# Sparse attention and a two-layer FFN: q and k on 128 partitions, one score phase, finer loads, stores on another queue

## The chip, the cores and the metric

The kernel runs on one core of a Trainium2 chip. The metric is the device time of one execution in microseconds, median of several runs. The profile gives the span from the first to the last instruction, which is some 2 us shorter than the device time here (313.7 us timed, 311.9 us span in the profiled run of the kernel before). A run that is over 1.5% above the fastest of its kernel counts as slow and is to be left out. Spans and lengths of stages are read from one profiled run per kernel.

The engines: PE (TensorE matmul), ACT (ScalarE), DVE (VectorE), POOL (GpSimd), SP (SyncE, here only a queue that issues DMA).

## The reference

```python
q, k, v: (8, 8, 576, 64)                    # batch, heads, tokens, head dim
rel = pos[:, None] - pos[None, :]
mask_local   = (rel >= 0) & (rel < 32)                        # heads 0 to 3
mask_strided = (rel >= 0) & (pos[None] % 32 == pos[:, None] % 32)   # heads 4 to 7
attn = softmax(where(mask, q @ k.T / 8, -1e9)) @ v
x    = attn as (8*576 tokens, 512)
out  = (((x @ w1) * (x @ w2)) @ w3) @ w_out                   # 512 -> 1024 -> 1024 -> 512
```

Both kernels fold `w3 @ w_out` into one matrix `w34` first, so that a token needs three products. Both compute only the blocks that the masks leave: six blocks of 96 queries by 128 keys for a local head, eight blocks of 72 by 72 for a strided head. Work is in fp16 with fp32 accumulation.

## The kernel before

The parts that the change and the argument touch, cut:

```python
LQ, LT = 96, 6          # local heads: 96 partitions, 6 tokens each
SQ, ST = 72, 8          # strided heads: 72 partitions, 8 tokens each
stgp = pool("stgp", bufs=5)                # fp32 staging, 8 KB slots
qkp  = pool("qkp", bufs=1)                 # cast q and k
psF  = pool("psF", bufs=3, PSUM)           # FFN and fold accumulators, one bank each
psB  = pool("psB", bufs=2, PSUM)           # scores and P*V, two banks each
psM  = pool("psM", bufs=1, PSUM)           # everything that is transposed, one bank

def load_w12():                            # 512 columns of w1 or w2 at a time
    ...
            nc.sync.dma_start(st, wd...)
            nc.scalar.copy(out=wh[:, 0:1, cs], in_=st[:, 0:1, :])
            nc.vector.tensor_copy(out=wh[:, 1:KM, cs], in_=st[:, 1:KM, :])

def ph_T(s, which):                        # one phase for q, one for k, of a head pair
    ps = psM.tile([P, 1024], FP16, tag="m")
    for c in range(n):                     # n = 6 or 8, w = 96 or 72
        pe(nc.tensor.transpose(ps[:, c * w:(c + 1) * w], src[:, c]..., id16[0:w, 0:w]))
    # one copy out of PSUM: q on ACT, k on DVE; POOL clears the pad behind k

def ph_S(s, g):                            # scores of half a pair's blocks, two phases a pair
    sps = psB.tile([P, 2, 512], FP32, tag="big")
    # m blocks x 2 heads: matmuls with 64 rows
    nc.scalar.activation(out=pte, in_=sps, func=AF.Exp, scale=scale)
    nc.vector.tensor_mul(ptm, pte, mask)

def ph_PV(s, g): ...                       # P*V, then reciprocal and product on DVE -> xqs
def ph_T2(s): ...                          # transposes xqs into xT, the FFN's input

# order of phases for pair p: S(p,0) Tq(p+1) S(p,1) T2(p-1) PV(p,0) Tk(p+1) PV(p,1)
# FFN tile t (512 tokens) is 16 first-layer units and 8 output units, four matmuls of
# 512 columns each; the phases of batch t+1 are laid between the units of tile t
```

The kernel keeps PE's instructions in program order (`pe(...)` in the listing), so a phase whose input is late holds up everything behind it. A "bank" below is a PSUM buffer of 2 KB a partition, as these pools allot them.

The softmax here doesn't subtract the row's maximum and nothing guards it: scores larger than these inputs give would overflow.

## Time and profile before

| | before |
|---|---|
| device time, median | 312.58 us (3 runs, 311.95 to 314.9) |
| first FFN matmul | 65.44 us |
| FFN tile 0 | 29.56 us |
| a steady FFN tile (tiles 1 to 5) | 28.71 us |
| first matmul of tile 7 (the last two tiles carry no attention) | 266.00 us |
| span | 311.9 us |

The starts of tiles are read from the timeline: the first `aps` matmul after an output unit.

Part 2 of the page, 40 slices of 7.8 us each; digits are tenths:

```profile
PE   0285757689999999999999999999999999999994
...
PEclk9999897569999999999999999999999999999999
DMA  6999999998769989999895868660002001102003
```

PE is full from the tenth slice on. Before that it is half empty, while the DMA engines are busy all the time (a share of 0.94 to 1.10 in every 10 us from 10 to 70 us), and the clock that PE is granted sinks to 0.5. At 0.5 the first unit of four FFN matmuls takes 1.71 us (65.64 us), at full clock 0.86.

The windows view of three stretches: the attention of batch 0, tile 0, a steady tile. Columns: stretch, its length, busy time (and count) of PE, PEld, DVE, ACT, POOL, then granted clock, DMA share, GB/s.

```profile
29.90:65.40 35.50, 24.89 (x282) 15.93 (x282) 24.71 (x44) 15.13 (x25) 12.55 (x24) 0.75 1.00 249
65.44:95.01 29.57, 29.57 (x296) 15.31 (x294) 20.95 (x40) 13.95 (x25) 17.82 (x27) 0.96 0.80 177
152.42:181.13 28.71, 28.45 (x298) 14.84 (x295) 20.52 (x41) 14.27 (x25) 11.95 (x21) 1.00 0.79 196
```

The chain of waits, start, length and what; first two links in the head, then three of a steady tile:

```profile
44.13 1.66 DVE w1h L141
56.35 1.66 DVE w2h L141
...
128.38 0.23 PE sps L224 x6
128.62 0.97 PE aps L294 x4
129.58 0.26 PE ps L201 x8
```

In the head, two casts of weights on DVE are links of the chain: batch 0's attention waits in the same queue. In the steady tile, all links are PE.

### The profile page before, as it was taken

The page shows a single profiled execution, that of the slowest core. Times are in us where ns is not written, and L with a number is a line of the kernel's source. Part 1 is how long each engine was busy: PE and PEld are TensorE (multiplying, and loading weights), DVE is VectorE, ACT ScalarE, POOL GpSimd, SP SyncE. Part 2 cuts the span into 40 slices and gives each one's busy share as a digit, 9 for nine tenths or more (in the row PEclk, how much of TensorE's full clock was granted, in tenths as well). Part 3 has the DMA queues.
Part 4 walks back from the last instruction along what each step waited for, and adds up shares of the span by engine and source line. Part 5 has one row for each costly group of instructions (what it writes and reads, how often), then busy time and mean ns, then how long its engine had stood idle before and what let it go on. Part 6 is the DMA issues. An engine that isn't in the chain of part 4 may idle for free.

```text
span 311.9 us, 6533 instructions
## 1 busy us (share of the span) xinstructions
PE 277.8 (89%) x2561; PEld 144.2 (46%) x2561; DVE 188.9 (61%) x361; ACT 134.6 (43%) x221; POOL 100.3 (32%) x192
## 2 busy tenths in 40 slices
PE   0285757689999999999999999999999999999994
PEld 0133334554554554555455554555554555444441
DVE  1234378868767676777678566778765666442421
ACT  2323435345545544544454455445544543332330
POOL 5041520557463364435356171733230000000000
PEclk9999897569999999999999999999999999999999
DMA  6999999998769989999895868660002001102003
GB/s 227 371 228 324 229 376 232 177 210 150 183 165 261 196 189 248 226 182 206 243 223 113 217 191 159 143 187 36 0 36 101 2 3 74 62 0 101 35 2 136
DMA packets 48287, 50.23 MB, mean 161 GB/s; under 512 B 26496, under 2 KB 32640, under 8 KB 48256
## 3 DMA queue, kind: packets, MB, share of 16 engines
q1 hardware_dynamic: 48256, 49.82, 63.1%
q8 instruction: 20, 0.33, 0.5%
q14 instruction: 11, 0.09, 0.1%
HBM read 40.37 MB, written 9.44 MB: 160 GB/s over the span
## 4 chain that ended last, share of the span: by engine, by line
PE 83%; DVE 6%; ACT 5%; DMA 3%; issue 1%; SPq 0%; DVEq 0%; ACTq 0%
PE ops L317 26%; PE bps L303 20%; PE aps L294 20%; PE ps L201 5%; PE sps L224 5%; PE xps L250 4%; DMA st<-in_moe_w_dram 3%; PE ps L266 3%; ACT pte L229 2%; DVE w_115 L350 1%; ACT xT_112 L273 1%; DVE w3T_117 L346 1%; DVE xqs L258 1%; PE ps L344 1%; DVE t L212 1%
## 5 line engine op out<-in xcount | busy, mean ns | idle before, releaser
L297 ACT COPY asb<-aps 128x512 f32<-128x512 f32 x72 | 42.2, 586 | 68.8 <-PE aps L294 51.3
L229 ACT ACTIVATE pte<-sps 128x576 f16<-128x576 f32 (+1 forms) x64 | 41.6, 650 | 36.7 <-PE sps L224 36.1
L173 POOL CAST t<-st 72x1024 f16<-72x1024 f32 x32 | 33.0, 1059 | 25.0 <-DMA st<-in_q_dram 15.1
L258 DVE TENSOR_TENSOR xqs<-xps,rcp 96x384 f16<-96x384 f32 (+1 forms) x64 | 39.6, 619 | 2.1
L154 POOL CAST t<-st 96x768 f16<-96x768 f32 x32 | 26.9, 867 | 29.2 <-DMA st<-in_q_dram 17.1
L303 PEld LDWEIGHTS <-w2h 128*128 128x128 f16 x288 | 24.5, 98 | 22.1 <-issue 1.3
L294 PEld LDWEIGHTS <-w1h 128*128 128x128 f16 x288 | 24.6, 99 | 21.9 <-issue 0.6
L201 PEld LDWEIGHTS <-t 72*128 72x128 f16 (+1 forms) x448 | 25.1, 101 | 17.0 <-issue 4.0
L201 PE MATMUL ps<-id_79,t 72*128 72x72 f16 (+1 forms) x448 | 28.5, 206 | 3.1 <-ACT w3T_118 L347 2.8
L250 PEld LDWEIGHTS <-ptm 72*128 72x128 f16 (+1 forms) x448 | 23.2, 101 | 17.2 <-issue 2.2
L236 DVE TENSOR_TENSOR ptm<-pte,maskS 72x576 f16<-72x576 f16 x32 | 19.3, 603 | 17.7 <-ACT pte L229 17.5
L294 PE MATMUL aps<-xT_112,w1h 128*128 128x512 f16 x72 | 27.5, 382 | 1.6 <-ACT xT_112 L273 1.5
L232 DVE TENSOR_TENSOR ptm<-pte,maskL 128x576 f16<-128x576 f16 x32 | 18.4, 576 | 16.2 <-ACT pte L229 15.6
L294 PE MATMUL aps<-xT_109,w1h 128*128 128x512 f16 x72 | 27.8, 386 | 0.0
L303 PE MATMUL bps<-xT_109,w2h 128*128 128x512 f16 x72 | 27.6, 384 | 0.0
L294 PE MATMUL aps<-xT_111,w1h 128*128 128x512 f16 x72 | 27.5, 382 | 0.0
L294 PE MATMUL aps<-xT_110,w1h 128*128 128x512 f16 x72 | 27.5, 382 | 0.0
L303 PE MATMUL bps<-xT_110,w2h 128*128 128x512 f16 x72 | 27.3, 379 | 0.0
L303 PE MATMUL bps<-xT_112,w2h 128*128 128x512 f16 x72 | 27.3, 379 | 0.0
L303 PE MATMUL bps<-xT_111,w2h 128*128 128x512 f16 x72 | 27.2, 378 | 0.0
L329 ACT COPY osb<-ops 128x512 f32<-128x512 f32 x18 | 10.5, 586 | 33.0 <-PE ops L317 33.0
L224 PEld LDWEIGHTS <-t 64*128 64x128 f16 x448 | 11.1, 97 | 29.1 <-issue 22.5
(89 smaller groups left out, 415.0 us busy)
## 6 DMA issues: line engine op xcount, KB each, us to landing
st<-in_q_dram SPq DMA_DIRECT2D x16, 576.0 KB
st<-in_k_dram SPq DMA_DIRECT2D x16, 576.0 KB
out_dram<-osb SPq DMA_DIRECT2D x36, 256.0 KB
st<-in_moe_w_dram SPq DMA_DIRECT2D x8, 1024.0 KB
st<-in_v_dram SPq DMA_DIRECT2D x32, 160.0 KB
st<-in_v_dram SPq DMA_DIRECT2D x8, 576.0 KB
st<-in_moe_w_out_dram SPq DMA_DIRECT2D x2, 1024.0 KB
st<-in_v_dram SPq DMA_DIRECT2D x8, 128.0 KB
```

Source lines behind the costliest of these rows:

```text
L154: nc.gpsimd.tensor_copy(out=t[:, hp], in_=stv[:, 2 * hp:2 * hp + 2].rearrange("p h c d -> p c h d"))
L173: nc.gpsimd.tensor_copy(out=t[:, hp], in_=stv[:, 2 * hp:2 * hp + 2].rearrange("p h c d -> p c h d"))
L201: pe(nc.tensor.transpose(ps[:, c * w:(c + 1) * w], src[:, c].rearrange("p h d -> p (h d)"), id16[0:w, 0:w]))
L224: pe(nc.tensor.matmul(sps[:, h, i * w:(i + 1) * w], s.tT["k"][r, ks:ks + P], s.tT["q"][r, w * t:w * t + w], start=True, stop=True))
L229: nc.scalar.activation(out=pte[0:kr], in_=sps[0:kr, :, 0:288], func=AF.Exp, bias=0.0, scale=scale)
L236: nc.vector.tensor_mul(ptm[0:kr, 0:576].rearrange("p (a x) -> p a x", x=w), pte[0:kr].rearrange("p h (a x) -> p (h a) x", x=w), _ap(maskS, ...
L250: pe(nc.tensor.matmul(xps[:, h, i * 65:(i + 1) * 65], ptm[0:kr, c0:c0 + P], vt[0:kr, 2 * (s.hp % 2) + h, g * m + i, :], start=True, stop=T ...
L258: nc.vector.tensor_mul(xqs[0:w, 0:m].rearrange("p i h d -> p h i d"), xv[:, :, :, 0:D], _ap(rcp, 0, [[rp, w], [4, 2], [1, m], [0, D]]))
L294: pe(nc.tensor.matmul(aps, w1h[:, ci, bass.ds(jc * P, P)], xT[ci][:, tok], start=(ci == 0), stop=(ci == KM - 1)))
L297: nc.scalar.copy(out=asb, in_=aps)
L303: pe(nc.tensor.matmul(bps, w2h[:, ci, bass.ds(jc * P, P)], xT[ci][:, tok], start=(ci == 0), stop=(ci == KM - 1)))
L317: pe(nc.tensor.matmul(st["ps"], lhs(ci), rhs(ci), start=(ci == 0), stop=(ci == KF - 1)))
```

## The change

Its intent: split every head's 576 tokens into 512, loaded as 4 tokens on each of 128 partitions, and a rest of 64. Then q and k of a pair, 512 columns each, fill the one PSUM bank that the kernel has for transposes (`psM`, 1024 fp16), and one phase transposes both. The rests of all heads are transposed once per batch. Scores become one phase a pair. Loads are cut to at most 512 KB over nine 4 KB slots, casts in the head are spread over ACT, DVE and POOL, cast q and k are double-buffered, and output tiles are copied by ACT and stored from ACT's queue. The core of the diff, cut:

```diff
-    stgp = ctx.enter_context(tc.tile_pool(name="stgp", bufs=5))
-    qkp = ctx.enter_context(tc.tile_pool(name="qkp", bufs=1))
+    stgp = ctx.enter_context(tc.tile_pool(name="stgp", bufs=9))
+    qkp = ctx.enter_context(tc.tile_pool(name="qkp", bufs=2))
...
+    def load_qk(b, grp, engs="pp"):
+        for nm, ten, eng in (("q", q, engs[0]), ("k", k, engs[1])):
+            st = stgp.tile([P, 4, 4, D], FP32, tag="stg")
+            nc.sync.dma_start(..., ten[b, 4 * grp:4 * grp + 4, 0:NM].rearrange("h (p c) d -> p h (c d)", c=4))
+            copy(eng, t, st.rearrange("p h c d -> p c h d"))
...
-    def ph_T(s, which):
+    def ph_T(s):
+        ps = psM.tile([P, 2, NM], FP16, tag="m")
+        for i, nm in enumerate("qk"):
+            for c in range(4):
+                pe(nc.tensor.transpose(ps[:, i, c * P:(c + 1) * P], ..., id16))
+        # then q out of it on ACT, k on DVE
+    def ph_R(b): ...                       # the 64 rest tokens of all heads: 4 transposes, 4 copies
-    def ph_S(s, g):
+    def ph_S(s):
+        for g in range(2):
...
-                if ts % 2 == 0:
-                    nc.scalar.copy(out=osb, in_=ps)
-                else:
-                    nc.vector.tensor_copy(out=osb, in_=ps)
-                nc.sync.dma_start(out_r[tch * (NT // P) + ts], osb)
+                nc.scalar.copy(out=osb, in_=ps)
+                nc.scalar.dma_start(out_r[tch * (NT // P) + ts], osb)
...
-    host(later, 14)
-    att_only(batch_end[0])
+    host(fold, 8, lead=14)                 # 14 fold units first, then 8 phases among the rest
+    host([lambda: None], batch_end[0])     # the rest of batch 0 alone
+    host(ab_halves(0), pos[0] + 6, lead=8) # 6 phases of batch 1 in the last 8 first-layer units
+    host(o_halves(0), batch_end[1])        # 15 or so in the 8 output units
```

Also cut: local v is loaded once and its overlapping rows are copied by DVE (`L180` below) instead of being loaded twice; masks shrink; pads are cleared once.

## The prediction

> **What bounds the kernel now.** From 65.6 us to the last matmul (307.8 us) TensorE is the limit. The windows view of one steady stage (one 512-token FFN tile with one batch of attention laid between, 28.7 us) shows PE busy 28.44 of 28.70 us, clock 1.00, DVE 20.0, ACT 14.3, POOL 13. In the chain of waits such a stage is PE throughout: 96 matmuls of 512 columns at 0.216 us = 20.7 us, and about 7.5 us of attention. The head, 0 to 65.6 us, is not PE-bound: its PE work is about 26 us (64 fold matmuls 13.8, fold transposes 3.6, one batch of attention 7.5, a start on the next), so some 39 us are lost. There the DMA share is 0.8 to 1.1 in every 10 us window, PE waits 8.4 us for the first w3 cast (first transpose at 13.05), the clock falls to 0.6 at 48 to 66 us, and the last w2 cast ends at 58. The load queue also waits for casts to free staging slots.
>
> **What the change does.**
> - Head: w3 first, in 512 KB pieces over nine small staging slots, w_out and w3 before q, k, v; casts spread over three engines; batch 1 after w1/w2. First transposes at about 6.5 us instead of 13, fold done by about 25. Needed before the first FFN tile: 10.5 MB of weights and 3.5 MB of batch 0. The trace moves 290 to 300 GB/s in 0 to 48 us (weights near 400, 72- and 96-partition loads 190 to 250), so 14 MB take 47 to 50 us. [...] Against that, q/k and w1/w2 packets shrink to 1 KB; by the trace's packet times I estimate 60 ns each, 290 GB/s.
> - Attention of batch 0 ends near 42 to 45 us, w1/w2 complete near 50; the first FFN tile starts at 46 to 48, fed in four pieces. Batch 1 lands after 60, so tile 0 carries 2 to 4 us of stalls.
> - Steady: columns transposed for q and k stay 4608 a batch, so PE saves only 0.1 us there; one score phase saves one of two 0.1 us entry gaps, 0.4 us a batch. 28.7 becomes about 28.2: 3.5 us over seven stages. POOL memsets, mask and copy changes are off the path. Output copies and store issues move to ACT (+1.2 us copies, about 1.6 us issue per stage): ACT near 60%, hidden.
> - Tail: 41.4 us for the last two tiles, plus 4 us, unchanged.
>
> **Sum.** Start of first tile 47 + 9 tiles 186 + seven batches at 7.1 = 50 + stalls 4 + tail 4 = 291 us. About 19 us of the gain is the head, 3 the stages.
>
> **What shows it right.** First FFN matmul at 45 to 52 us; first transpose before 8; stages of 28.0 to 28.4; DMA share above 0.9 until about 60 us; fewer clock drops in the head. [...] this trace has 0.5 at 54 to 68 us, where PE is sparse.
>
> **What makes it wrong.** 1 KB packets slower than estimated; batch 1 starved in tile 0; ACT blocked behind a store; the score phase waiting for both PSUM buffers; slow POOL casts delaying batch 0.
>
> Faster by over 2% 0.94, within 2% 0.05, slower 0.01; range 281 to 302.

Beside its two estimates, the profile of the kernel before shows these numbers: for 60 ns a packet, 48256 packets that took 63.1% of 16 engines' span of 311.9 us, 65 ns on average at 1.03 KB; for 1.6 us of issue a stage (four stores), 0.33 us in the median and 0.82 at most for one issue.

## The result, and the profile after

The changed kernel takes 301.51 us (4 runs, 300.88 to 302.47) against 313.27 us for the kernel before in the same rounds (4 runs). The ratio is 0.9625, 95% interval 0.9568 to 0.9682. Ratios here are the mean time of one kernel's fast runs over that of the other's fast runs of the same rounds, so not quite the ratio of the medians.

It is faster, as forecast, and the time lies in the range, but only 0.5 us below its upper end and 10.5 us above the point.

| stage (us) | before | sum in the prediction | after |
|---|---|---|---|
| first FFN matmul | 65.44 | 47 | 51.10 |
| tile 0 | 29.56 | 20.7 + 7.1 + 4 = 31.8 | 36.12 |
| tiles 1 to 6 | 170.99 | 6 x 27.8 = 166.8 | 165.94 |
| last two tiles and tail | 45.9 | 41.4 + 4 | 45.4 |
| span | 311.9 | 291 | 298.5 |
| time of the profiled run | 313.7 | 291 | 300.9 |

So the start of the FFN is 4.1 us later than predicted and tile 0 is 4.3 us longer; the steady tiles are right to a microsecond, the tail too. The last 2.4 us are the step from span to time, which the sum left out.

The page's part 2 after:

```profile
PE   1396677999889999999999999999999999999995
...
PEclk9999995899999999999999999999999999999999
DMA  7999997696289998997699894120011002003003
```

PE is full from the eighth slice, sags once at slices 11 and 12, and the clock sinks for two slices instead of four. The windows view after: fold, attention of batch 0, tile 0, a steady tile (columns as before):

```profile
12.16:27.10 14.94, 13.66 (x88) 7.56 (x88) 6.74 (x13) 7.23 (x10) 3.97 (x5) 1.00 1.15 317
27.10:51.10 24.00, 16.33 (x208) 10.34 (x208) 18.94 (x41) 11.45 (x19) 7.33 (x8) 0.85 1.01 288
51.10:87.22 36.12, 32.03 (x308) 17.06 (x306) 25.67 (x52) 19.88 (x36) 17.02 (x18) 0.96 0.71 176
170.96:198.79 27.83, 27.53 (x277) 14.93 (x274) 19.42 (x42) 15.14 (x30) 9.25 (x10) 1.00 0.49 124
```

The stretch of batch 0's attention takes 24.0 us instead of 35.5. The two don't hold quite the same work: the stretch before also has 32 matmuls of the fold and the first phases of batch 1 (PE busy 24.9 us), the one after 24 matmuls of the fold (PE busy 16.3 us). Tile 0 is 8.3 us longer than a steady tile. The scores in the chain of waits of a steady tile:

```profile
176.72 0.36 PE sps L246 x12
177.08 0.97 PE bps L319 x4
```

Twelve score matmuls in 0.36 us and one slowed group behind them, where before six took 0.23 us and each six had its slowed group.

The timeline in tile 0 shows what is new. Columns: start, length, engine, line, operation, count, and in brackets how long the engine had been idle and what ended it. `ps` is the bank for transposes; the 4 transposes at L228 are those of the rests.

```profile
61.27 0.61 PE L212 MATMUL ps<-id_79,t 128*128 128x128 f16 x8
...
61.91 0.58 ACT L68 COPY qT<-ps 128x512 f16<-128x512 f16 x1 [0.72 <-PE ps L212]
...
62.53 0.69 DVE L70 COPY kT<-ps 128x512 f16<-128x512 f16 x1 [0.30 <-ACT qT L68]
...
63.27 0.38 PE L228 MATMUL ps<-id_79,t 128*128 128x128 f16 x4 [0.54 <-DVE kT L70]
```

(L68, L70 and L72 are the lines of a helper that copies on ACT, DVE and POOL; the names of the tiles tell the copies apart.) The copy of k starts only when that of q has ended (0.62 us after it started), and the next transposes wait for the copy of k. The two copies read different halves of the same PSUM bank. It is so in the whole trace: of 15.8 us that DVE sat idle before such copies in this kernel, 15.3 ended with ACT's copy of q. Why the second copy waits was not shown, since no run gave q and k a bank each; with the layout that lets them share one, their copies run in series.

The first transposes did come early, at 5.32 us. The timeline shows what became of that:

```profile
5.32 1.04 PE L355 MATMUL ps<-id_79,t 128*128 128x128 f16 x8 [2.25 <-POOL t L72]
...
10.46 0.69 DVE L70 CAST woh<-st 128x1024 f16<-128x1024 f32 x1 [1.85 <-DMA st<-in_moe_w_out_dram]
11.07 0.42 DVE L357 COPY w3T_129<-ps 128x512 f16<-128x512 f16 x1
...
12.16 1.01 PE L355 MATMUL ps<-id_79,t 128*128 128x128 f16 x8 [5.80 <-ACT w3T_130 L358]
```

DVE has two casts of w_out ahead of the copy of those transposes and waits for their loads. PE's second block starts at 12.16 us; the first block of the kernel before started at 13.06.

### The profile page after: what moved, and what is told of

The parts are those of the page before. It is cut to its first block, busy times and chain, and to the rows that moved or that the text cites. A ratio compares the mean times of both kernels' runs of the same rounds, so it can differ in the third digit from the quotient of the medians.

```text
span 298.5 us, 6146 instructions
## 1 busy us (share of the span) xinstructions
PE 269.3 (90%) x2401; PEld 143.0 (48%) x2401; DVE 183.5 (61%) x382; ACT 145.7 (49%) x256; POOL 86.5 (29%) x102
## 4 chain that ended last, share of the span: by engine, by line
PE 62%; DMA 18%; DVE 7%; ACT 6%; POOL 3%; issue 3%; SPq 1%; POOLq 0%; ACTq 0%
PE ops L333 17%; PE bps L319 16%; PE aps L310 15%; DMA st<-in_v_dram 10%; PE xps L266 4%; PE ps L212 3%; DMA st<-in_moe_w_out_dram 3%; DMA out_dram<-osb 3%; PE sps L246 2%; DMA st<-in_k_dram 2%; DVE kT L70 2%; ACT qT L68 2%; PE ps L282 2%; DVE xqs L274 1%; ACT pte L251 1%
## 5 line engine op out<-in xcount | busy, mean ns | idle before, releaser
L72 POOL CAST t<-st 128x1024 f16<-128x1024 f32 (+1 forms) x40 | 39.7, 994 | 74.6 <-DMA st<-in_q_dram 29.6
L251 ACT ACTIVATE pte<-sps 128x576 f16<-128x576 f32 (+1 forms) x64 | 38.3, 648 | 11.0 <-PE sps L246 11.0
L68 ACT COPY qT<-ps 128x512 f16<-128x512 f16 (+1 forms) x48 | 22.8, 481 | 31.9 <-PE ps L212 27.4
L344 ACT COPY osb<-ops 128x512 f32<-128x512 f32 x36 | 21.1, 585 | 28.5 <-PE ops L333 28.5
L70 DVE COPY kT<-ps 128x512 f16<-128x512 f16 (+1 forms) x48 | 25.2, 538 | 15.8 <-ACT qT L68 15.3
L310 PE MATMUL aps<-xT_121,w1h 128*128 128x512 f16 x72 | 27.6, 384 | 0.0
L212 PE MATMUL ps<-id_79,t 128*128 128x128 f16 x256 | 19.5, 219 | 1.7 <-ACT w3T_130 L358 1.3
L212 PEld LDWEIGHTS <-t 128*128 128x128 f16 x256 | 16.5, 98 | 9.1 <-issue 2.5
L272 DVE RECIPROCAL rcp<-xps 96x6 f32<-96x6 f32 (+1 forms) x64 | 12.2, 190 | 12.6 <-PE xps L266 12.3
L282 PEld LDWEIGHTS <-xqs 72*128 72x128 f16 (+1 forms) x224 | 12.5, 100 | 9.8 <-issue 2.0
L282 PE MATMUL ps<-id_79,xqs 72*128 72x72 f16 (+1 forms) x224 | 14.5, 206 | 2.8 <-DVE kT L70 1.9
```

Of the source, the lines that this page charges most:

```text
L68: nc.scalar.copy(out=out, in_=in_)
L70: nc.vector.tensor_copy(out=out, in_=in_)
L72: nc.gpsimd.tensor_copy(out=out, in_=in_)
L212: pe(nc.tensor.transpose(ps[:, i, c * P:(c + 1) * P], src[:, c, h0:h0 + 2].rearrange("p h d -> p (h d)"), id16))
L251: nc.scalar.activation(out=pte[0:kr], in_=sps[0:kr, :, 0:288], func=AF.Exp, bias=0.0, scale=scale)
L282: pe(nc.tensor.transpose(ps[:, t * w:(t + 1) * w], s.xqs[t // m][0:w, t % m].rearrange("p h d -> p (h d)"), id16[0:w, 0:w]))
```

## The experiments

Twelve more kernels were run. All but two (e6 and e12) give the right result. Starts and lengths of tiles are from each run's timeline.

| run | first FFN matmul | tile 0 | tiles 3 to 5, each | span | ratio to before |
|---|---|---|---|---|---|
| changed kernel | 51.10 | 36.12 | 28.12, 27.84, 27.83 | 298.5 | 0.9625 |
| e1_spread | 50.88 | 35.73 | 28.03, 27.83, 27.83 | 298.5 | 0.9576 |
| e2_two_scores | 51.10 | 34.25 | 28.89, 28.89, 28.89 | 302.8 | 0.9717 |
| e3_stores_sp | 50.01 | 36.33 | 27.61, 27.83, 27.61 | 297.8 | 0.9578 |
| e4_single_casts | 51.25 | 36.56 | 28.21, 27.83, 27.83 | 299.2 | 0.9592 |
| e5_old_layout | 50.00 | 37.37 | 28.12, 31.77, 27.91 | 304.7 | 0.9761 |
| e6_quarter_w12 | 57.00 | 36.28 | 27.83, 27.83, 27.83 | 304.9 | one look |
| e7_batch0_first | 53.11 | 34.70 | 28.57, 27.84, 27.83 | 299.4 | 0.9652 |
| e8_two_m | 47.05 | 34.48 | 28.54, 28.36, 27.87 | 298.1 | 0.9570 |
| e9_shared_banks | 47.38 | 35.78 | 27.83, 27.83, 27.83 | 295.0 | 0.9384 |
| e10_shared_batch0 | 56.68 | 34.76 | 28.22, 27.83, 27.83 | 303.7 | 0.9588 |
| e11_relief | 47.20 | 35.87 | 27.83, 27.83, 27.83 | 295.2 | 0.9374 |
| e12_light_pool | 46.64 | 33.21 | 27.83, 27.93, 27.83 | 292.3 | 0.9405 |

The intervals of the ratios reach about 0.003 to 0.009 to either side, and the chips differ, so ratios less than one per cent apart are not told apart here. By the two per cent rule every kernel with a ratio is faster than the kernel before, except e5, which is unclear (0.9706 to 0.9815). In the rounds of e9 to e11 the record lists three of the seven runs of the kernel before as slow, and the ratios seem to include them; against the four fast ones e9 is 0.944, which is still below the changed kernel's interval.

Stage lengths in the profiles repeat to a few hundredths of a microsecond where PE is full, and tell more. Starts and spans repeat less well. The four timed runs of one kernel have spans that differ by 0.7 us (e8) to 5.0 us (e10); for the changed kernel they run from 298.5 to 300.3. The profile is one of these runs: the fastest for the changed kernel and e12, the slowest for e9, e10 and e11. A difference of a microsecond or two in a start or a span is therefore weak evidence. Tile 0 also holds a stretch at half clock whose length varies: 3.1 us in the changed kernel, none in e7, 6.1 us in e10.

### e1_spread: is batch 1's attention squeezed into too few units?

```diff
-    host(ab_halves(0), pos[0] + 6, lead=8)
+    host(ab_halves(0), pos[0] + 12, lead=2)
```

> The changed kernel with batch 1's attention laid from the second unit of FFN tile 0 on (12 of its phases in the first 14 units left, the rest in the output half) instead of 6 phases in the last 8 units. In the changed kernel tile 0 takes 36.1 us (51.1 to 87.2) against 27.8 for a later tile. Theory A, the attention is squeezed: 15 phases between 8 output units wait for each other's copies, so spreading them makes tile 0 about 30 to 32 us and the span 4 to 6 us shorter (about 293). Rival B, batch 1's data come late: the PE then waits for q, k and v inside the first half of tile 0 instead, and tile 0 stays at 35 to 37 us.

Measured: tile 0 takes 35.73 us, the span is the same 298.5. Theory A fell: more units between the phases bought nothing. Rival B is not borne out either: PE's waits in tile 0 name no load. The main ones are these (engine, line, waited for: us, times, longest):

```profile
PE xps L266 <- DVE ptm L253: 1.4, 2, 0.9
PE ps L212 <- DVE kT L70: 1.4, 2, 1.2
PE ps L228 <- DVE kT L70: 1.1, 1, 1.1
```

The copy of k out of the shared bank, and the mask product `ptm` on DVE. Both became the next theories.

### e2_two_scores: what is one score phase worth?

```diff
-            add(ph_S, pairs[p])
+            add(ph_S, pairs[p], (0,))
+            add(ph_S, pairs[p], (1,))
```

(with `ph_S` taking the groups as an argument, and the counts of phases before tile 0 and in it raised to match)

> The changed kernel with the scores in two phases again. Theory: one phase saves one entry gap of PE, 0.09 us a pair, 0.36 us a batch; so a steady tile goes from 27.84 to about 28.2 us, and the span by 2.5 to 3 us to 301 to 302. Rival: the steady gain (28.71 to 27.84) is from elsewhere (q/k layout or stores), and the steady tile stays below 27.95.

Measured: a steady tile takes 28.89 us instead of 27.83, so one score phase is worth 1.05 us a tile, not the 0.36 expected. The chain of waits of this run:

```profile
177.41 0.23 PE sps L246 x6
177.65 0.97 PE aps L310 x4
178.62 0.23 PE sps L246 x6
178.85 0.97 PE bps L319 x4
```

Two phases cost 2 x (0.23 + 0.11 that the unit behind is longer) = 0.68 us a local pair; one costs 0.36 + 0.11 = 0.47. That is 0.21 us a pair, 0.84 a batch. The other 0.2 us of a tile are a wait at its start, for ACT's copy of `xT`; in the waits view over four tiles, first e2, then the changed kernel:

```profile
PE aps L310 <- ACT xT L289: 2.0, 4, 0.5
PE aps L310 <- ACT xT_124 L289: 1.2, 4, 0.3
```

The prediction had counted one 0.1 us a pair. There are two: of the second group's 0.23 us only 0.13 are work (0.36 less 0.23), and the unit behind it is 0.11 longer. Scores use 64 rows, the FFN matmuls before and behind them 128; this trace puts the cost of going from one to the other at about 0.1 us on each side. What causes it was not shown.

Tile 0 tells the opposite: with two score phases it takes 34.25 us, 1.9 less than in the changed kernel, at the same start and with as long a stretch at half clock. So the single phase wins 1.05 us in every steady tile and loses some of it where PE waits for ACT and DVE; on the span it is worth 4.3 us.

### e3_stores_sp and e4_single_casts: stores and the double buffer

```diff
-                nc.scalar.copy(out=osb, in_=ps)
-                nc.scalar.dma_start(out_r[...], osb)
+                if ts % 2 == 0: nc.scalar.copy(...)
+                else: nc.vector.tensor_copy(...)
+                nc.sync.dma_start(out_r[...], osb)
```

> The changed kernel with the output tiles copied by ACT and DVE in turn and stored from the queue that also issues the loads, as before. Theory: stores and copies lie off the path in a steady tile; 27.84 us a tile stays within 0.15 us, and the span within 1.5 us of 298.5 (perhaps shorter, as ACT has less to do). Rival: the split of the queues matters, loads wait behind stores, and steady tiles lengthen by over 0.3 us.

```diff
-    qkp = ctx.enter_context(tc.tile_pool(name="qkp", bufs=2))
+    qkp = ctx.enter_context(tc.tile_pool(name="qkp", bufs=1))
```

> The changed kernel with one buffer instead of two for the cast q and k. Theory: loads and casts run far ahead of the attention in steady tiles, so nothing there changes (27.84 within 0.15); batch 1's casts must wait for batch 0's transposes, which are long over, so the span stays within 1 us of 298.5. Rival: the double buffer carries part of the gain, and the span grows by 2 us or more.

Measured: 297.8 and 299.2 us of span, steady tiles of 27.6 to 27.8 us and 27.8. Neither part carries any of the gain that can be seen. e4 stays within what its theory said. e3 does nearly: two of its steady tiles are 27.61 us, 0.23 shorter than 27.84 where 0.15 was allowed, and tile 1 is longer, 28.53 us instead of 27.78.

### e5_old_layout: what is the layout worth?

```diff
-            st = stgp.tile([P, 4, 4, D], FP32, tag="stg")        # 128 partitions, 4 tokens
+                st = stgp.tile([w, 2, n * D], FP32, tag="stg")   # 96 x 6 or 72 x 8, two heads
-    def ph_T(s):  ...
+    def ph_T(s, nm): ...          # q and k in two phases, as before; no ph_R
```

(eight staging slots instead of nine, because the cast tiles of this layout are larger)

> The changed kernel with q and k loaded and transposed as before (96 and 72 partitions, a transpose phase each for q and k, none for the rest), one staging slot less so that it fits. Theory: the layout is worth 0.1 to 0.3 us in a steady tile, and shows in the head, where each phase costs a copy: tile 0 then starts at 53 to 57 us instead of 51.1, the span is 4 to 8 us longer. Rival: the head is bound by what is loaded; the layout moves fewer packets per byte before, so the head does not change by over 1 us.

Measured: the first FFN matmul at 50.0 us, a microsecond earlier, so the layout is not what shortened the head; tile 0 at 37.37, 1.25 us longer. Tile 1 takes 28.90 us, 1.1 more; tiles 2, 3 and 5 take 27.9 to 28.25 us, up to 0.4 more. The span is 6.2 us longer, of which 3.9 are in one tile. The timeline shows it:

```profile
174.14 0.59 ACT L324 COPY osb<-ops 128x512 f32<-128x512 f32 x1 [1.46 <-DMA out_dram<-osb]
...
175.32 0.38 PE L290 MATMUL aps<-xT,w1h 128*128 128x512 f16 x1 [1.86 <-ACT xT L269]
```

ACT waited for an earlier store to free an output buffer, the copy of `xT` stood behind it in ACT's queue, PE stood still for 1.86 us, and the clock was at half for the next 3.4 us. This is the "ACT blocked behind a store" of the prediction. It did not happen in the changed kernel; whether the layout or chance brought it on is open, since this is one profile.

### e6_quarter_w12: does loading bound the start of the FFN?

```diff
+            if g == 0:
+                w12st[eng] = consts.tile([P, KM, 256], FP32, name="w12st" + eng)
+                nc.sync.dma_start(w12st[eng], ...)
-            copy(eng, wh[:, :, cs], st)
+            copy(eng, wh[:, :, cs], w12st[eng])
```

> Wrong result on purpose: only the first quarter of w1 and w2 is loaded and cast four times, 3 MB less to load in the head (one staging slot less, so that it fits). If loading bounds the start of the first FFN tile, it starts some 8 to 10 us earlier than 51.1. If the chain of batch 0's attention does, it stays within 1.5 us of 51.1; batch 1's data would then land some 8 us earlier, and tile 0 is shorter than 36.1 us only if it was starved by them.

Measured: with 3 MB less to load, the first FFN matmul came 5.9 us later, at 57.0. So less to load did not help. The timeline shows what came in its place (the casts of all four groups are ready at once, and go first):

```profile
46.57 3.88 ACT L68 CAST w1h<-w12sta 128x1024 f16<-128x1024 f32 x4
...
50.14 2.48 DVE L70 CAST w2h<-w12stv 128x1024 f16<-128x1024 f32 x4
...
53.89 0.62 PE L269 MATMUL xps<-v16S,ptm 72*128 72x65 f16 x8 [2.60 <-DVE ptm L256]
```

Casts of weights sit in the queues of ACT and DVE ahead of the last steps of batch 0's attention. POOL adds to it: it casts batch 1 earlier, and batch 0's eight mask products on DVE take 7.8 us instead of 4.0 (e12 shows why). This run does not separate the two.

What the bound is in the changed kernel itself, its own timeline shows:

```profile
44.56 1.05 ACT L68 CAST w1h<-st 128x1024 f16<-128x1024 f32 x1
...
51.10 0.62 PE L310 MATMUL aps<-xT_121,w1h 128*128 128x512 f16 x1
```

The first quarter of w1 was loaded and cast by 45.6 us (that of w2 by 47.9), and PE began the first FFN unit at 51.1, right behind the last transposes of batch 0's attention. Loading is not the bound of the start.

In the changed kernel, the late arrival of w1 and w2 keeps most of their casts out of the chain. The fault of e6 resembles the 1.7 us casts in the chain of the kernel before: there DVE spent 4 x 1.73 us between 29.9 and 65.4 us on w1 and w2; after, 1.4 us between 27.1 and 51.1. That this is a large part of the head's gain is an inference from this run, not shown by one of its own. Tile 0 stayed at 36.28 us although batch 1's loads had 3 MB less ahead of them. The clock was at half for the first 5 us of it, 2 us longer than in the changed kernel, which hides about 1 us; so late data can't be more than a small part of its 8 us.

### e7_batch0_first: attention under the fold

```diff
-    load_w3(0, "p")
-    ...                                   # w_out, w3, then batch 0
+    load_qk(0, 0, "av"); load_rest(0, "a")
+    ...                                   # w_out, w3 0-1, v, w3 2-3, q and k of heads 4-7, ...
+    host([lambda: None], 3)
-    host(fold, 8, lead=14)
+    host(fold, batch_end[0] - 3, lead=2)
```

> The changed kernel with batch 0's q and k loaded ahead of w_out and w3, v and the second half of the heads between the w3 pieces, and the fold units laid between the attention phases of batch 0. Of the head, 12 to 27 us is fold alone (PE-bound, 2.17 us a block) and 27 to 51 us a chain of batch 0's attention through ACT and DVE. Theory: the two can run side by side, the first FFN matmul comes at 42 to 46 us instead of 51.1, and the span is 4 to 8 us shorter. Rival, loading is the bound (14 MB by 47 us): the first FFN matmul stays at 50 or later. Against the theory: the quarter-load run showed that work put between the phases on ACT and DVE lengthens the chain.

Measured: the first FFN matmul at 53.1 us, two later; the clock was never halved; the span is 0.9 us longer. The theory fell in this form. PE's longest waits were 4.6 us for casts of w3, which now come later, 2.7 us for a cast of q, and 2.8 and 2.6 us for copies of k out of the transpose bank, which the fold needs too.

### e8_two_m and e9_shared_banks: the transpose bank

```diff
-    psF = pool(name="psF", bufs=3, PSUM)      # e8: 2
-    psM = pool(name="psM", bufs=1, PSUM)      # e8: 2
+    psF = pool(name="psF", bufs=4, PSUM)      # e9: one set of four
+    psM = psF                                 # and tag "f" for transposes too
```

> The changed kernel with two PSUM banks for transposes instead of one, and two instead of three for FFN accumulators. In the changed kernel q and k of a pair share one bank, their copies run one after the other (0.59 then 0.69 us) and the next transpose waits for the second. Theory: that wait is a part of the 5 us lost in tile 0 (36.1 us) and of the 24 us chain of batch 0; with two banks tile 0 starts 1 to 2 us earlier and is 1 to 3 us shorter, while steady tiles may lengthen as the accumulators have less room. Rival: the chain waits for ACT and DVE being busy, not for the bank; then start and length of tile 0 stay within 0.7 us.

Measured: tile 0 starts at 47.05 us, 4.05 earlier, and is 1.64 us shorter. The theory holds, and is larger than it said for the start. Tile 1 is 1.4 us longer, tiles 2 to 4 each 0.4 to 0.5, and tile 7, which has no attention, 22.0 instead of 21.0, so the span gains only 0.4. Accumulators had become a scarce buffer: in e8's waits view PE waits 1.8 us in five places for DVE's product, which reads `bps` and so frees it; that of the changed kernel lists no such wait.

> The changed kernel with its four single PSUM banks (three for FFN accumulators, one for transposes) made one rotating set of four. With two fixed transpose banks the first tile started 4 us earlier and was 1.6 us shorter, and steady tiles were 0.5 us longer for want of accumulators. Theory: the set gives both: start at 46 to 48 us, tile 0 at 33.5 to 35, steady tiles at 27.7 to 28.0, span 292 to 294. Rival: a rotating set makes a tile wait for the oldest one whatever its kind, so steady tiles stay at 28.3 or longer and nothing is won.

Measured: start 47.38, tile 0 35.78, steady tiles 27.83, span 295.0. The rival fell: a rotating set costs the steady tiles nothing from tile 2 on (tile 1: 28.57). Start and steady tiles came as expected, tile 0 did not (33.5 to 35 expected), and the span missed its range by one microsecond. In the timeline the wait for the copy of k is gone (same columns as above):

```profile
57.82 0.61 PE L212 MATMUL ps<-id,t 128*128 128x128 f16 x8
...
58.47 0.58 ACT L68 COPY qT<-ps 128x512 f16<-128x512 f16 x1 [0.72 <-PE ps L212]
...
59.08 0.69 DVE L70 COPY kT<-ps 128x512 f16<-128x512 f16 x1 [0.30 <-ACT qT L68]
59.13 0.39 PE L228 MATMUL ps<-id,t 128*128 128x128 f16 x4
```

The two copies still run in series, but the rests' transposes start at 59.13 us while k is being copied. The start of the FFN moved by about what such waits had cost: between 27.1 and 51.3 us of the changed kernel PE's transposes wait 3.4 us in all for copies out of the one bank (1.4 and 0.7 for k, 1.3 for w3), and in e9 none of these waits is left. The windows view of the run, batch 0's attention and tile 0:

```profile
27.10:47.40 20.30, 14.40 (x197) 9.44 (x198) 17.70 (x41) 10.92 (x19) 6.50 (x7) 0.84 1.09 295
47.38:83.16 35.78, 32.16 (x308) 17.03 (x306) 26.48 (x49) 18.71 (x34) 17.98 (x20) 0.95 0.95 207
```

The time is 296.64 us (4 runs, 295.68 to 297.38), ratio 0.9384, 95% interval 0.9337 to 0.9432: clear of the changed kernel's interval. Its four spans, 293.3 to 295.0 us, are clear of the changed kernel's, 298.5 to 300.3, too. This version gives the right result and beats both kernels.

### e10_shared_batch0 and e11_relief: what is left of the head

e10 is e7's order with e9's banks. e11 is e9 with two groups of casts moved off DVE:

```diff
-    load_rest(0, "v")
+    load_rest(0, "p")
-        for wd, wh, eng in ((moe_w1, w1h, "a"), (moe_w2, w2h, "v")):
+        for wd, wh, eng in ((moe_w1, w1h, "a"), (moe_w2, w2h, "p")):
```

> The rotating set of four banks, with batch 0 loaded first and the fold laid between its phases. With one transpose bank that order moved the first FFN matmul to 53.1 us, later than 51.1. Theory: fold blocks and attention phases shared the one transpose bank and held each other up; with the set the first FFN matmul comes at 44 to 47 us, with the clock not halved, and the span is 1 to 4 us below that of the set alone. Rival: DVE and ACT are the bound of the head (DVE 18.9 of 24 us busy between 27 and 51 us), and the order does not matter: the same start within 1 us.

> The rotating set of four banks, with DVE relieved in the head: the casts of w2 and of batch 0's remainder rows on POOL instead. Takes 3.5 to 4 us of work off DVE between 28 and 59 us. If DVE's load bounds the chain of batch 0 and tile 0, the start and the length of tile 0 together shrink by 1.5 to 4 us against the set alone; if the latency of the chain does, by under 1 us; and POOL's slower casts (1.04 us and more against 0.68) may delay w2 and batch 1 instead.

Measured: e10 starts the FFN at 56.68 us, 9.3 later than e9. Neither theory nor rival. The longest entry of its waits view is for DVE's casts of w3:

```profile
PE ps L355 <- DVE t L70: 9.0, 3, 5.2
```

So the order of loads does matter, and this one is bad. (The profile is the slowest of its four runs, with spans of 298.7 to 303.7 us; so 9.3 may be some microseconds too many, but the fastest run is still 3.7 us longer than the slowest of e9.) Whether another order could lay the fold under the attention is open. e11 starts at 47.20 us with a tile 0 of 35.87: no change of over 0.2 us. In tile 0 DVE is busy 23.4 us instead of 26.6, and the tile is no shorter (its half clock lasts 1.3 us longer, which hides 0.6), so there DVE's load is not the bound. In the stretch before it the run tests little: DVE's busy time fell only from 17.6 to 17.1 us, because beside POOL's new casts the mask products took 520 ns on average instead of 453 and the copies of v rows 676 instead of 325. That the time from step to step bounds that chain is likely, but not shown.

### e12_light_pool: what stretches tile 0?

```diff
-            nc.gpsimd.tensor_copy(out=vt[:, 2 * hp:2 * hp + 2, :, 0:D], in_=st)
+            w = 1 if b in (1, 2) else D
+            nc.gpsimd.tensor_copy(out=vt[:, 2 * hp:2 * hp + 2, :, 0:w], in_=st[:, :, :, 0:w])
```

(and so for POOL's other casts of batch 1's v and batch 2)

> Wrong result on purpose: the rotating set of four banks, with POOL casting only one column of batch 1's v and of batch 2's q, k, remainder and v (loads unchanged, ACT, DVE and PE work unchanged but for two short extra fills at the start). In the set's trace the mask product on DVE takes 454 ns when no POOL cast overlaps it and 779 ns on average when one does, and tile 0 (35.8 us against 27.8) has PE waits of about 4.7 us, most of them for that product, besides 1.7 us of half clock and 1.1 us of extra transposes. Theory: POOL's casts stretch the DVE work of tile 0; without them the mask products there all take about 455 ns, and tile 0 is 33 to 34 us, the span 2 to 3 us shorter. Rival: the latency of the chain alone does it, tile 0 stays within 0.7 us of 35.8.

Measured: in the profiles tile 0 takes 33.21 us, 2.6 less, and the span is 2.7 us shorter; tile 1 is 0.5 longer. The timed runs do not confirm the gain in the span: it compares the slowest of e9's four runs with the fastest of e12's, whose spans reach 296.2 us, the chips differ, and the intervals of the two ratios overlap. What follows rests on tile 0 and on the durations. (The waits view names 3.9 us of PE's waits in e9's tile 0, not the 4.7 of the expectation.) The groups of DVE from 51 to 83 us (tile 0; in e12 also the first 3 us of tile 1), first e9, then e12; columns: line, operation, output and inputs, shape, count, busy us, mean ns of one, idle before:

```profile
L253 DVE TENSOR_TENSOR ptm<-pte,maskL 128x576 f16<-128x576 f16 x4 | 3.1, 797 | 0.1
L253 DVE TENSOR_TENSOR ptm<-pte,maskS 72x576 f16<-72x576 f16 x4 | 2.7, 684 | 0.5 <-ACT pte L251 0.5
L180 DVE COPY v16L<-v16L 32x640 f16<-32x640 f16 x3 | 2.4, 812 | 0.1
```

```profile
L261 DVE TENSOR_TENSOR ptm<-pte,maskL 128x576 f16<-128x576 f16 x6 | 2.6, 454 | 0.1
L261 DVE TENSOR_TENSOR ptm<-pte,maskS 72x576 f16<-72x576 f16 x4 | 1.8, 450 | 0.7 <-ACT pte L259 0.7
L187 DVE COPY v16L<-v16L 32x640 f16<-32x640 f16 x4 | 1.3, 324 | 0.1
```

The same product takes 450 to 454 ns with POOL nearly idle and 684 to 797 with POOL casting; the copy of v rows 324 against 812. Over all 64 mask products of the changed kernel, the 41 with no POOL cast beside them took 453 ns on average, the 23 others 784. Of these 23, the seven that began before the cast took 442 to 459 ns; the 16 that began inside a cast ended 0.30 to 0.32 us after the cast did, as if they had waited for its end. One of them, from the timeline of the changed kernel (the cast ends at 69.38 us, the product at 69.69):

```profile
68.15 1.23 POOL L72 CAST t<-st 128x1024 f16<-128x1024 f32 x1 [1.26 <-DMA st<-in_k_dram]
...
68.56 1.13 DVE L253 TENSOR_TENSOR ptm_106<-pte,maskL 128x576 f16<-128x576 f16 x1
```

A part of the 2.6 us, some 0.5, is that the clock came back earlier in this run (2.6 us of tile 0 at half clock instead of 3.7).

## Why the prediction was right or wrong

**Direction and range: right; the split between head and stages only in its order.** The span fell by 13.4 us: 14.3 from the start of the FFN, 5.1 from tiles 1 to 6, 0.5 from the end, less 6.6 that tile 0 gave back. The point was 10.5 us too low, and these terms make that up: start 4.1, tile 0 4.3, and 3.0 from leaving out the step from the span (298.5) to the median time (301.5), less 0.9 in the steady tiles. "About 19 us of the gain is the head, 3 the stages" was 14.3 and 5.1, and of the 14.3 tile 0 gave 6.6 back. That the range held is in part luck: the two terms that missed most, the start and tile 0, had the wrong mechanism, and only 0.5 us were left.

**"14 MB take 47 to 50 us", hence "start of first tile 47": the wrong bound.** The rate was right (317 and 288 GB/s in the windows of the head), but the weights for the first unit were cast by 47.9 us and PE began it at 51.1; e6 took 3 MB away and the start came later; e8 and e9 left the loads as they are and it came 4 us earlier. What bounds the start is the chain of batch 0's attention, 27.1 to 51.1 us, and the FFN cannot begin before it ends. The prediction had that chain end "near 42 to 45 us" and took the load for the limit. The chain is long because each step passes through ACT or DVE, because casts share their queues, and because one PSUM bank serves all transposes: e8 and e9 gave it more banks and the start moved to 47.1 and 47.4. The change itself brought a part of this in: q and k in one bank are copied one after the other. One term of the loading was also mis-sized: while w1 and w2 arrive in packets of 1 KB, 35 to 44 us, the trace moves 348 GB/s, not 290. What the number of partitions of a load does to its rate was not tested; in the kernel before, the trace moves 242 GB/s while loads of 96 partitions arrive (13.5 to 17.5 us) and 218 while those of 72 do (28 to 33 us).

What shortened the head by 14.3 us is known by exclusion only. Without the single score phase, the store queue, the double buffer or the layout the start stays at 50.0 to 51.3 us (e2 to e5). What is left, the order and size of the loads, the spread of the casts and the fold laid ahead of the attention, was not taken apart.

**"First transposes at about 6.5 us, fold done by about 25": the first half was right (5.32), and worth little.** The copy of those transposes stood behind casts of w_out on DVE, and PE's second block began at 12.16. The last fold matmul was at 39.6.

**"Tile 0 carries 2 to 4 us of stalls", because "batch 1 lands after 60": the size and the cause were wrong.** Tile 0 is 8.3 us longer than a steady tile. By the starts of matmuls, this is about 1.6 us of work that only tile 0 carries (31 more matmuls: the transposes of both ends and one more score phase), 1.4 of half clock ((1 - 0.96) x 2 x 36.12 us at half speed, half of it lost), and some 5 us for the rest. Of these the waits view names 4.2 us of PE's waits, all for ACT's and DVE's results. Batch 1's loads are not among them (e1, e6). Three causes were tried, each with one profile, and they overlap, so that they can't be added: POOL's casts, which slow DVE's mask products, about 2 us (e12); the single score phase, 1.9 us (e2); the bank, 1.6 us in e8 and 0.3 in e9. How the 5 us divide among them stays open.

**"One score phase saves one of two 0.1 us entry gaps, 0.4 us a batch": the gap was there, the term was mis-sized.** It is 0.21 us a pair in the chain, since entering and leaving cost 0.1 us each, and 1.05 us a tile by e2. The text of the prediction therefore had 28.2 us a tile, and 27.8 was measured. The sum came out right by luck, since it used 20.7 + 7.1 = 27.8, which did not agree with its own text.

**"PE saves only 0.1 us" from the layout, stores hidden on ACT: right.** Undoing the layout costs 0 to 0.4 us in tiles 2, 3 and 5 (e5; 1.1 in tile 1), undoing the stores or the double buffer nothing that can be seen (e3, e4). The memsets and masks were not tried.

**"Fewer clock drops": right.** The clock of batch 0's stretch rose from 0.75 to 0.85, but it was still at half when the first FFN unit ran (0.50 from 43.96 to 54.2 us; the first FFN matmuls start 0.43 us apart, later ones 0.22). PE was not idle before the clock fell, but sparse: in the 3.4 us before 43.96 us it was busy 2.03 us, in the two stretches of 3.4 us before that, at full clock, 2.98 and 2.74 us. At what share the clock falls was not shown. Of the other signs, "DMA share above 0.9 until about 60 us" did not come (0.94 from 40 to 50 us, 0.73 from 50 to 60).

## What to carry to other kernels

When a stage is bound by a chain across engines, count what else stands in those engines' queues and which single buffer every link passes through: casts that arrive early can lengthen it, in the same queue or beside it on POOL (in e6 the start came 5.9 us later), and a bank shared in rotation can shorten it (a span of 295.0 against 298.5 us here) where a fixed split only moves the wait (298.1). Packing q and k into one PSUM bank saved a phase here, but their copies on two engines ran in series (0.58, then 0.69 us). Before blaming a transfer for a late start, look when its data were ready, then take a part of it away and see whether the start moves, and what the earlier data set off.
